# Chunk-selecting attention and a gated FFN on one core: first blocks as 128-token half units, v of the first blocks cast by POOL's DMA queue in one chain with the weights

## The chip, the cores and the metric

The kernel runs on one core of a Trainium2 chip. The metric is the device time of one execution in microseconds; three executions of the kernel before took 316.68, 316.73 and 319.05, median 316.73. A profiled execution gives the trace. Five engines work side by side, each through its own instructions in order: TensorE (PE, matmuls), VectorE (DVE), ScalarE (ACT), GpSimd (POOL) and SyncE (SP, which here only issues DMAs). ACT and POOL issue DMAs too.

## The reference

Inputs are q, k, v of shape (4, 8, 768, 64) in float32 and the weights of a gated FFN (512 to 1536 to 512). Cut to what matters:

```python
k_min, k_max = min and max of k over each chunk of 32 tokens
ub = sum_d max(q * k_min, q * k_max)            # an upper bound per query and chunk
ub = where(chunk of query >= chunk, ub, -1e9)
selected = the 6 chunks of the largest ub
scores = q k^T / 8, masked to selected chunks and to past tokens
attn = softmax(scores) v                        # (4, 8, 768, 64)
x = attn with heads side by side: 3072 tokens x 512
xn = x / sqrt(mean(x^2) + 1e-6) * rms_g
g = xn w_gate;  out = (g * sigmoid(g) * (xn w_val)) w_out
```

A query among the first 128 tokens of a sequence sees at most 4 chunks, so all that it sees are selected.

## The kernel before

The work is cut into 12 blocks of 256 tokens: batch b and block m (0, 1, 2) of its sequence, in the order of the list ORDER (L369, the blocks with m = 0 of all batches first). Each block has two jobs, one for each group g of four heads, then a normalization (`norm`) and an FFN (`ffn`). Block 0 alone (SPLIT) runs its FFN as two pieces of 128 tokens, with its scores cut to match.

A job (`job`) does this. DVE transposes k and q in 32 x 32 squares (L512); ACT or POOL makes bf16 copies of them (L519, L520). DVE reduces k to the minimum and maximum of each chunk (L527); POOL or DVE places these in a block-diagonal tile BD (L539). TensorE multiplies q and its positive part with BD, which gives the bound ub (`upper`, L574). DVE transposes it, takes the sixth largest value (L598) and makes a mask, which a matmul with chunkrow adds to the scores (L654). TensorE computes scores (L643) with the keys on the partitions, ACT the exponential (L693), POOL the triangle of the diagonal blocks (L663). The values matmul (L719) takes v from VX, a bf16 tile with a column of ones, which ACT or POOL casts from vraw (L625, L626). DVE divides by the sum (L734, L738).

`norm` squares the rows on ACT (L754), takes the root on POOL (L760, L762), scales on DVE (L769), transposes on TensorE (L779) and copies with rms_g on DVE or ACT (L788, L792). `ffn` runs gate and value matmuls (L817), 256 tokens wide or, for a piece of 128, with 128 columns and the same number of matmuls; tanh on ACT (L824), products on DVE (L828) and POOL (L839) into hh; or, for some, the last product on DVE (L832). The projection (L849) needs all hh of its tokens and all three thirds of wo. Its result is halved and stored.

k and q come by DMAs on the SP queue (for block 0 half of them on ACT's), v on SP's; each of wg, wv and wo comes in thirds, nine transfers on POOL's queue with a cast to bf16. HELD makes the first load of blocks 2 and 3 wait until a weight third has landed. SP works its issues off in order, so a wait holds the issues behind it, stores among them.

The order of all engines is not written out by hand. A planner (class Plan) gets every operation with an engine or a choice of engines (`flex`), a duration, a priority (due time: attention of a block LEAD = 60 us ahead of its FFN, blocks PACE = 23 us apart), what it reads and writes, and the buffers that it takes. It lists the operations in the order in which they would start. Where TensorE would wait in the first 60 us, it puts matmuls of an identity (L903) that keep it busy.

Of the kernel before, what the change touches and what calls it, by code (L numbers as in the profile page):

```python
# [21 lines left out]
class Op:  # L22
    __slots__ = ("eng", "occ", "lat", "fn", "pri", "deps", "waits", "done",
                 "takes", "uses", "dma", "ready", "mode", "start", "name", "seq", "users", "alts", "after", "inst")

    def __init__(self, name, eng, occ, lat, fn, pri):
        self.name, self.eng, self.occ, self.lat, self.fn, self.pri = name, eng, occ, lat, fn, pri
        self.deps, self.takes, self.uses, self.users, self.after = [], [], [], [], []
        self.dma = None
        self.mode = None  # L30
        self.done = None
        self.alts = {eng: (occ, lat, fn)}


class Rings:
# [34 lines left out]
    def add(self, t, ring, packets, cost, op):  # L70
        self._step(min(t, self.wait[0][0]) if self.wait else t)

        def landed(now, op=op):
            op.done = now + (0.9 if op.dma[2] else 1.2)
        op.done = None
        self.wait.append((t, ring, [packets, cost, landed]))
        self.wait.sort(key=lambda w: w[0])
        self.guess()
# [28 lines left out]
class Plan:  # L107
# [3 lines left out]
    SHARES = ("scale", "swap", "relu", "bd0", "bd1", "dk", "mk")  # L111
    HOP = {"PE": 0.055, "ACT": 0.04, "DVE": 0.04, "POOL": 0.075, "SP": 0.06}
# [37 lines left out]
    def run(self, in_order=(), fill=None):  # L150
# [25 lines left out]
        def est(o, e):  # L176
            t = at[e]
# [28 lines left out]
        while todo:  # L206
            best = None
            for e, c in cand.items():
# [4 lines left out]
                if not rows:  # L213
                    continue
                t0 = max(at[e], min(t for t, o in rows))
                t, o = min(((t, o) for t, o in rows if t <= t0 + 1e-9),
                           key=lambda r: (r[1].pri, r[1].seq))
# [7 lines left out]
            if e == "PE" and fill is not None:  # L225
                begin, cold, end, step, pool, fn = fill
                t0 = max(begin, at[e])
                f = [x for x in self.free[pool] if x[0] + 0.055 <= t0]
# [21 lines left out]
            if o.dma is not None:  # L250
                packets, cost, hw = o.dma
                rings.add(t + o.occ + (0.6 if hw else 1.4), e, packets, cost, o)
# [26 lines left out]
def kernel(  # L279
# [41 lines left out]
    def at(key):  # L321
# [4 lines left out]
    buffers("vraw", 2, [P, 2, NG, 4, D], FP32)  # L326
# [3 lines left out]
    buffers("VX", 20, [P, 2, 4, D + 1], BF16)  # L330
    buffers("qb", 5, [P, 2, BLK], BF16)
    buffers("kx", 3, [P, 2, 2, CB], FP32)
# [13 lines left out]
    buffers("hh", 13, [P, 512], BF16)  # L346
# [22 lines left out]
    ORDER = [(0, 0), (1, 0), (2, 0), (3, 0), (0, 1), (1, 1), (0, 2), (2, 1), (1, 2),  # L369
             (3, 1), (2, 2), (3, 2)]  # L370
    assert sorted(ORDER) == [(b, m) for b in range(B) for m in range(NBLK)]
    PACE, LEAD = 23.0, 60.0
    SPLIT = {0}
    PACKED = {0, 1, 2}
    DIRECT = {(i, hp) for i in range(len(ORDER)) for hp in range(KH) if i >= 6 and hp % 2}

    def HALVES(i):
        return ((0,), (1,)) if i in SPLIT else ((0, 1),)

    def due_attn(i):  # L380
        return PACE * i - LEAD

    def due_ffn(i):
        return PACE * i

    def dma(name, eng, src, dst, packets, cost, pri, writes, takes=(), reads=(), behind=()):
# [11 lines left out]
        o.dma = (packets, cost, eng != "POOL")  # L398
        return o
# [8 lines left out]
    def constants():  # L408
# [25 lines left out]
        for i, t in enumerate(store["VX"]):  # L434
            plan.op(f"ones{i}", "POOL", 0.035, 0.14, lambda t=t: GE.memset(t[:, :, :, D:D + 1], 1.0),
# [6 lines left out]
    HELD = {2: (("wv", 2), ("wo", 1)), 3: (("wo", 1), ("wo", 2))}  # L442

    def load_qk(i, nm, src):
        b, m = ORDER[i]
        key = (nm + "raw", b, m)
        first = True
        for n, a in enumerate((0, 2, 1, 3)):
            eng = ("SP", "ACT")[n % 2] if i == 0 else "SP"
            rows = slice(32 * a, 32 * (a + 1))  # L450
            if i in PACKED:
                sv = src[b].rearrange("(g a) (m r j) d -> a m r g (j d)", a=4, m=NBLK, r=32)[a, m]
                todo = [(sv, lambda rows=rows: at(key)[rows].rearrange("r g j h d -> r g (j h d)"),
                         4, 0.098)]
            else:
                todo = []
                for g in range(NG):
                    sv = src[b, 4 * g + a, BLK * m:BLK * (m + 1), :].rearrange(
                        "(j r) d -> r j d", r=32)
                    todo.append((sv, lambda rows=rows, g=g: at(key)[rows, g].rearrange(  # L460
                        "r j h d -> r j (h d)"), 16, 0.019))
            for k_, (sv, dst, packets, cost) in enumerate(todo):
                dma(f"load {nm}{b}{m}{a}{k_}", eng, sv, dst, packets, cost,
                    loads_due(i, nm == "q"), writes=[key],
                    takes=[(key, nm + "raw")] if first else (),
                    behind=[HELD[i][0]] if i in HELD and first else ())
                first = False

    def loads_due(i, n):
        return -500 + 10 * i + n if i < 2 else due_attn(i) - 30 + n  # L470

    def load_v(i):
        b, m = ORDER[i]
        key = ("vraw", b, m)
        for e in range(2):
            t0 = BLK * m + P * e
            dma(f"load v{b}{m}{e}", "SP", v[b, :, t0:t0 + P, :].rearrange("a p d -> p a d"),
                lambda e=e: at(key)[:, e].rearrange("p g a d -> p (g a) d"),
                64, 0.02, loads_due(i, 2 if i != 1 else -1), writes=[key],
                takes=[(key, "vraw")] if e == 0 else (),  # L480
                behind=[HELD[i][1]] if i in HELD and e == 0 else ())

    def load_w(n, pri, **kw):
        for w, src, nm in ((wg, moe_w_gate, "wg"), (wv, moe_w_val, "wv")):
            dma(f"{nm}{n}", "POOL", src[:, n * TH:(n + 1) * TH].rearrange("(kt p) n -> p kt n", p=P),
                lambda w=w: w[:, :, n * TH:(n + 1) * TH], 32, 0.081, pri, writes=[(nm, n)], **kw)

    def load_wo(n, pri):
        r = slice(n * 4, n * 4 + 4)
        dma(f"wo{n}", "POOL", moe_w_out.rearrange("(kt p) n -> p kt n", p=P)[:, r],  # L490
            lambda: wo[:, r], 32, 0.081, pri, writes=[("wo", n)])

    first_dk = []


    def job(i, g):
        b, m = ORDER[i]
        J = (b, m, g)
        w = 64 if m == 0 else BLK
        nj = w // 64  # L500
        base = due_attn(i) + 0.5 * g
        early = i < 2
        kraw, qraw, vraw = ("kraw", b, m), ("qraw", b, m), ("vraw", b, m)
        kT, qT, kb, qb, kx = ("kT", *J), ("qT", *J), ("kb", *J), ("qb", *J), ("kx", *J)
        bd = ("BD", b, g)

        def turn(nm):
            raw, T = (nm + "raw", b, m), (nm + "T", *J)
            fast = i not in PACKED
            tokens = "p h (j r) -> p j h r" if fast else "p h (r j) -> p j h r"  # L510
            plan.op(f"turn {nm}{J}", "DVE", 0.6 if fast else 0.94, 0.7 if fast else 1.10,
                    lambda: VE.transpose(out=at(T).rearrange(tokens, r=32, j=8),  # L512
                                         in_=at(raw)[:, g]),
                    base + (0 if nm == "k" else 1), reads=[raw],
                    writes=[T], takes=[(T, nm + "T")])

        def half(nm):
            T, hb = (nm + "T", *J), (nm + "b", *J)
            act = lambda: SE.activation(out=at(hb), in_=at(T), func=ACT.Copy)  # L519
            pool = lambda: GE.tensor_copy(at(hb), at(T))  # L520
            flex(f"half {nm}{J}", {"ACT": (0.54, 0.63, act), "POOL": (0.57, 0.61, pool)},
                 base + 2, reads=[T], writes=[hb], takes=[(hb, nm + "b")])
# [3 lines left out]
        for n, op in enumerate((ALU.min, ALU.max)):  # L526
            plan.op(f"ext{n}{J}", "DVE", 0.585, 0.67, lambda n=n, op=op: VE.tensor_reduce(  # L527
                out=at(kx)[:, n], in_=at(kT).rearrange("p h (c t) -> p h c t", t=CH),
                axis=AXX, op=op), base + 1, reads=[kT], writes=[kx],
                takes=[(kx, "kx")] if n == 0 else ())  # L530
        def sub(eng):
            return lambda: eng.tensor_tensor(
                out=at(kx)[:, 1], in0=at(kx)[:, 1], in1=at(kx)[:, 0], op=ALU.subtract)

        first_dk.append(flex(f"dk{J}", {"POOL": (0.175, 0.22, sub(GE)), "DVE": (0.1, 0.16, sub(VE))},
                             base + 2, reads=[kx], writes=[kx]))
        for n in range(2):
            def place(eng, n=n):
                return lambda: eng.tensor_tensor(  # L539
                    out=BD[b, g].rearrange("p t (h c) -> p t h c", h=2)[  # L540
                        :, 2 * n:2 * n + 2, :, CB * m:CB * (m + 1)],
                    in0=at(kx)[:, n].unsqueeze(2).to_broadcast([P, 2, 2, CB]),
                    in1=own[:].unsqueeze(1).to_broadcast([P, 2, 2, CB]), op=ALU.mult)

            flex(f"bd{n}{J}", {"POOL": (0.21, 0.255, place(GE)), "DVE": (0.11, 0.17, place(VE))},
                 base + 2, reads=[kx, "own", bd], writes=[bd, bd + (m,)])
        turn("q")
        half("q")
        qR = ("qR", *J)

        def qr():
            return at(qraw)[:, g].rearrange("p j h d -> p (j h d)")[:, 0:2 * w].rearrange(
                "p (h s) -> p h s", h=2)

        def relu(eng):
            return lambda: eng.tensor_scalar(
                out=qr(), in0=at(qT)[:, :, BLK - w:], scalar1=HUGE, scalar2=0.0,
                op0=ALU.min, op1=ALU.max)
# [378 lines left out]
```

## Time and profile before

| what | value |
|---|---|
| median of three executions | 316.73 us |
| profiled execution | 321.97 us |
| its span in the trace | 320.3 us |
| mean granted TensorE clock in it | 0.989 |
| PE, DVE, ACT, POOL busy | 302.4, 220.5, 216.2, 156.4 us |
| DMA packets | 30.66 MB, of them POOL's queue 4.72 MB |

How to read it: a line of a group gives line, engine, operation, output and inputs by the program's names, count, busy time, mean of one, and the idle time of the engine just before with what ended it. A line of the timeline begins with the start and the length in microseconds. PE's busy time counts pipelined matmuls that overlap, and filler. The profiled execution is about 5 us above the median; its clock fell below full in two stretches.

### The profile page before, as it was taken

To read this page: it belongs to the slowest core of one execution; us is meant where nothing else is said; L and a number is where in the kernel's file an instruction comes from. 1 tells how busy PE (TensorE), PEld (TensorE's weight loads), DVE (VectorE), ACT (ScalarE), POOL (GpSimd) and SP (SyncE) were. 2 spreads that over 40 slices of the span, in tenths; PEclk is the share of its full clock that TensorE was granted. 3 is DMA by queue.
4 is the path that set the end of the run, shared out by engine and by line. 5 is a ranking of instruction groups with operands and counts; after the bars stand their busy time and mean duration, and the time that the engine had idled before them with its cause. 6 is when DMAs were issued, how large, how long until landed. Compare 5 with 4: busy or idle time off the path is not lost.

```text
span 320.3 us, 11960 instructions
## 1 busy us (share of the span) xinstructions
PE 302.4 (94%) x4952; PEld 235.4 (73%) x4952; DVE 220.5 (69%) x599; ACT 216.2 (68%) x393; POOL 156.4 (49%) x287
## 2 busy tenths in 40 slices
PE   8788999979998999879999999999999999999994
PEld 8687886865865877656788687788587688678681
DVE  6877499895998998968956836496465366437360
ACT  2566746974768896496797686679579469665240
POOL 4774493876764777488656353155133114213120
PEclk9999999998999999979999999999999999999999
DMA  8999986576564647775310300100010110010101
GB/s 183 220 239 207 251 160 150 112 197 142 149 134 118 141 109 174 163 165 114 99 39 19 115 5 2 68 3 4 33 37 0 36 37 2 36 35 2 65 2 65
DMA packets 74838, 30.66 MB, mean 96 GB/s; under 512 B 65568, under 2 KB 70176, under 8 KB 74784
## 3 DMA queue, kind: packets, MB, share of 16 engines
q1 hardware_dynamic: 69712, 24.66, 31.5%
q0 software_dynamic: 4752, 4.72, 8.9%
q8 instruction: 39, 0.64, 0.8%
q10 hardware_dynamic: 320, 0.52, 0.6%
q14 instruction: 15, 0.12, 0.1%
HBM read 28.31 MB, written 6.29 MB: 108 GB/s over the span
## 4 chain that ended last, share of the span: by engine, by line
PE 69%; DVE 8%; DMA 7%; SPq 7%; ACT 4%; issue 3%; POOL 1%; DVEq 0%; ACTq 0%
PE F L817 30%; PE F L849 17%; SPq L390 6%; PE F L719 6%; PE S L643 6%; PE S L574 4%; DMA kraw<-in_k_dram 3%; DMA qraw<-in_q_dram 3%; PE S L654 2%; PE F L903 2%; DMA vraw<-in_v_dram 2%; DVE kx L527 2%; PE F L779 1%; DVE tg L828 1%; ACT pt L693 1%
## 5 line engine op out<-in xcount | busy, mean ns | idle before, releaser
L693 ACT ACTIVATE pt<-S 128x1024 bf16<-128x1024 f32 (+3 forms) x100 | 86.2, 887 | 25.8 <-PE S L654 24.8
L839 POOL TENSOR_TENSOR hh<-tg,vs 128x512 bf16<-128x512 bf16 x54 | 62.3, 1157 | 64.1 <-ACT vs L836 40.7
L828 DVE SCALAR_TENSOR_TENSOR tg<-th,F 128x512 bf16<-128x512 bf16 x72 | 48.8, 681 | 44.1 <-ACT th L824 37.9
L817 PE MATMUL F<-xsT,wg 128*128 128x256 bf16 (+1 forms) x624 | 76.0, 267 | 1.7 <-DVE xnat L738 1.7
L817 PE MATMUL F<-xsT,wv 128*128 128x256 bf16 (+1 forms) x624 | 75.8, 266 | 0.5 <-DVE tg L828 0.5
L849 PE MATMUL F<-wo,hh 128*128 128x512 bf16 x288 | 68.2, 381 | 0.0
L817 PEld LDWEIGHTS <-wg 128*128 128x128 bf16 x624 | 56.4, 99 | 10.8 <-issue 2.7
L817 PEld LDWEIGHTS <-wv 128*128 128x128 bf16 x624 | 55.8, 98 | 8.1 <-issue 1.0
L824 ACT ACTIVATE th<-F 128x512 bf16<-128x512 f32 x72 | 43.0, 602 | 15.0 <-PE F L817 13.5
L663 POOL TENSOR_SCALAR_AFFINE_SELECT pt<-pt 128x512 bf16<-128x512 bf16 x48 | 31.2, 654 | 42.8 <-ACT pt L693 42.4
L849 PEld LDWEIGHTS <-hh 128*128 128x128 bf16 x288 | 26.5, 98 | 27.9 <-issue 0.8
L643 PE MATMUL S<-qb,kb 32*128 32x256 bf16 (+1 forms) x784 | 33.3, 257 | 3.3 <-ACT pt L693 2.0
L836 ACT ACTIVATE vs<-F 128x512 bf16<-128x512 f32 x54 | 32.4, 600 | 4.4 <-PE F L817 3.3
L527 DVE TENSOR_REDUCE kx<-kT 128x16 f32<-128x512 f32 x48 | 30.8, 663 | 0.0
L719 PE MATMUL F<-VX,pt 128*128 128x65 bf16 x672 | 26.9, 195 | 3.7 <-ACT vs L836 3.0
L719 PEld LDWEIGHTS <-pt 128*128 128x128 bf16 x672 | 24.9, 99 | 6.0 <-ACT pt L693 2.3
L865 DVE TENSOR_SCALAR osb<-F 128x512 f32<-128x512 f32 x17 | 11.6, 687 | 24.7 <-PE F L849 24.6
L643 PEld LDWEIGHTS <-kb 32*128 32x128 bf16 x784 | 14.0, 92 | 15.5 <-issue 13.7
L903 PE MATMUL F<-ident 128*128 128x128 bf16 x328 | 23.1, 232 | 2.1 <-POOL ident masks.py:199 1.4
L903 PEld LDWEIGHTS <-ident 128*128 128x128 bf16 x328 | 20.8, 105 | 2.8 <-POOL ident masks.py:199 1.4
L654 PE MATMUL S<-mtd,chunkrow 32*128 32x128 bf16 (+2 forms) x384 | 20.9, 204 | 0.6 <-issue 0.6
L654 PEld LDWEIGHTS <-chunkrow 32*128 32x128 bf16 x768 | 19.3, 94 | 2.4 <-issue 1.4
(60 smaller groups left out, 374.4 us busy)
## 6 DMA issues: line engine op xcount, KB each, us to landing
vraw<-in_v_dram SPq DMA_DIRECT2D x24, 256.0 KB, 4.2
out_dram<-osb SPq DMA_DIRECT2D x24, 256.0 KB, 2.1
kraw<-in_k_dram SPq DMA_DIRECT2D x72, 64.0 KB, 2.8
qraw<-in_q_dram SPq DMA_DIRECT2D x72, 64.0 KB, 2.3
wg<-in_moe_w_gate_dram POOLq DMA_DIRECT2D x3, 512.0 KB, 11.9
wv<-in_moe_w_val_dram POOLq DMA_DIRECT2D x3, 512.0 KB, 11.6
wo<-in_moe_w_out_dram POOLq DMA_DIRECT2D x3, 512.0 KB, 17.5
kraw<-in_k_dram SPq DMA_DIRECT2D x10, 128.0 KB, 5.4
```

The lines of the kernel that those rows point to most:

```text
L527: plan.op(f"ext{n}{J}", "DVE", 0.585, 0.67, lambda n=n, op=op: VE.tensor_reduce(out=at(kx)[:, n], in_=at(kT).rearrange("p h (c t) -> p h c ...
L643: TE.matmul(s[a // 2][:, a % 2, c0:c0 + q1 - q0], kbt[r, t, ks], qbt[r, t, q0:q1], start=(t == 0), stop=(t == 1 and not mask), skip_group_ ...
L654: TE.matmul(o, chunkrow[r, BLK * kg + P * e:BLK * kg + P * (e + 1)], mv, start=False, stop=(d == 1), skip_group_check=True)
L693: lambda pt=pt, hs=hs, c0=c0, c1=c1, x=sc[hp]: SE.activation(out=at(pt)[:, hs, c0:c1], in_=at(x)[:, :, c0:c1], func=ACT.Exp, scale=SCALE), ...
L719: TE.matmul(o[:, a, :], p_[:, a, off:off + P], vt[:, e, a, :], start=(kb_ == 0 and a == 0), stop=(kb_ == nkb - 1 and a == 3), skip_group_c ...
L817: TE.matmul(at(p_)[:, n * W:(n + 1) * W], w[:, g, ht * P:(ht + 1) * P], at(xT)[:, g, 0:W], start=(g == 0), stop=(g == NP - 1), skip_group_ ...
L824: plan.op(f"tanh{U}.{hp}", "ACT", 0.48, 0.6, lambda th=th, gp=gp: SE.activation(out=at(th), in_=at(gp), func=ACT.Tanh, scale=0.5), pri, re ...
L828: VE.scalar_tensor_tensor(out=at(tg), in0=at(th), scalar=1.0, in1=at(gp), op0=ALU.add, op1=ALU.mult), pri - 30, reads=[th, gp], writes=[tg ...
L836: plan.op(f"vcopy{U}.{hp}", "ACT", 0.48, 0.6, lambda vs=vs, vp=vp: SE.activation(out=at(vs), in_=at(vp), func=ACT.Copy), pri + 0.1, reads= ...
L839: plan.op(f"hh{U}.{hp}", "POOL", 1.11, 1.16, lambda tg=tg, vs=vs, hh=hh: GE.tensor_tensor(out=at(hh), in0=at(tg), in1=at(vs), op=ALU.mult) ...
L849: TE.matmul(at(op)[:], at(("hh", *U, ht // K))[:, o:o + P], wo[:, ht, :], start=(ht == 0), stop=(ht == NHT - 1))
L903: TE.matmul(store["F"][slot][:, 0:P], ident[:], ident[:], start=True, stop=True)
```

## The change

The list of blocks becomes a list of units. The four blocks with m = 0 are cut into halves of 128 tokens: first the first halves of all four batches, then their second halves, then the eight other blocks whole, in the order of before. A first half needs no bound and no mask; its chunk minima and maxima are computed all the same, but with a due time of the second half. Each half runs its own norm and its own FFN piece with 128 columns. SPLIT is gone; instead the last unit's norm and FFN run in two pieces.

Loads of k and q for the first eight units are one DMA for each head group, with 128 partitions and runs of 1 KB, and a job waits only for its own group. They follow each other on SP in one line (FIRST), unit 0's q on ACT's queue. v of the eight half units isn't loaded to vraw any more: POOL's queue copies and casts it straight into VX. These eight casts and the nine weight thirds form one chain on that queue in the order CAST; for the planner each starts no earlier than 3.5 us before the transfer two ahead is done (AHEAD, `follow`). v0 waits for unit 0's k, the first weights for its q. Loads k3, k4, k5, k6 wait for weight thirds (HELD).

Buffers: vraw 2 to 1, VX 20 to 10 of double size, kx 3 to 8, six new ones kh for half k, hh 13 to 12. The planner gets PATIENT, which on DVE lets a more urgent operation that is soon ready go ahead of a long one; it assumes later SP loads to land 1.5 us later; and the buffers xs and hh are no longer handed out in strict order. A gate matmul waits for both wg and wv of its third.

```diff
+    AHEAD = 3.5
+    PATIENT = {"DVE": 0.6}
...
-            t = at[e]
+            t = max(at[e], o.floor)
+            if o.follow is not None:
+                t = max(t, o.follow.done - self.AHEAD)
...
+                if e in self.PATIENT:
+                    soon = [r for r in rows if r[0] <= t0 + self.PATIENT[e]]
+                    for t, o in now + sorted(soon, key=lambda r: (r[1].pri, r[1].seq)):
+                        end = t + o.alts[e][0] - 0.1
+                        if not any(t < r[0] < end and r[1].pri < o.pri - 10 for r in soon):
+                            break
...
-    buffers("vraw", 2, [P, 2, NG, 4, D], FP32)
+    buffers("vraw", 1, [P, 2, NG, 4, D], FP32)
...
-    buffers("VX", 20, [P, 2, 4, D + 1], BF16)
+    buffers("VX", 10, [P, 2, 2 * 4, D + 1], BF16)
...
-    buffers("kx", 3, [P, 2, 2, CB], FP32)
+    buffers("kh", 6, [P, 2, P], FP32)
+    buffers("kx", 8, [P, 2, 2, CB], FP32)
...
-    buffers("hh", 13, [P, 512], BF16)
+    buffers("hh", 12, [P, 512], BF16)
...
-    ORDER = [(0, 0), (1, 0), (2, 0), (3, 0), (0, 1), (1, 1), (0, 2), (2, 1), (1, 2),
-             (3, 1), (2, 2), (3, 2)]
+    LATE = [(0, 1), (1, 1), (0, 2), (2, 1), (1, 2), (3, 1), (2, 2), (3, 2)]
+    UNITS = [(b, 0, (t,)) for t in range(2) for b in range(B)] + [(b, m, (0, 1)) for b, m in LATE]
...
-    SPLIT = {0}
-    PACKED = {0, 1, 2}
-    DIRECT = {(i, hp) for i in range(len(ORDER)) for hp in range(KH) if i >= 6 and hp % 2}
+    PACKED = {i for i, (b, m, toks) in enumerate(UNITS) if m == 0}
+    DIRECT_FROM = 10
...
+    def pieces(i):
+        toks = UNITS[i][2]
+        return tuple((t,) for t in toks) if i == len(UNITS) - 1 else (toks,)
...
+        o.slack = 1.5 if pri > -30 and eng == "SP" else 0.0
...
-    HELD = {2: (("wv", 2), ("wo", 1)), 3: (("wo", 1), ("wo", 2))}
+    FIRST = "k0 q0 k1 q1 k2 q2 k3 q3 k4 q4 k5 q5 k6 q6 k7 q7".split()
+    CAST = "v0 v1 w0 v2 w1 v3 w2 wo0 v4 wo1 v5 wo2 v6 v7".split()
+    HELD = {"k3": ("wg", 0), "k4": ("wv", 2), "k5": ("wo", 0), "k6": ("wo", 1)}
+    START = {"v0": ("k", 0), "w0": ("q", 0)}
...
+    def cast_v(i, **kw):
+        b, m, toks = UNITS[i]
+        key, e = ("VX", b, m), toks[0]
+        t0 = BLK * m + P * e
+        dma(f"cast v{i}", "POOL", v[b, :, t0:t0 + P, :].rearrange("a p d -> p a d"),
+            lambda: at(key)[:, e, :, 0:D], 64, 0.022, -400, reads=[key] + ones + kw.pop("reads", []),
+            writes=[key + ("h", e)], takes=[(key, "VX")] if not e else (), **kw)
...
+        w = BLK if m else 64 * s0
...
+        later = base if whole or s0 else due_attn(UNIT_OF[b, m, 1]) + 0.5 * g
...
-        base = due_ffn(i) + toks[0]
+        base = due_ffn(i) + (11.5 if toks[0] and m else 0)
...
-                            reads=[xT, (nm, third)], writes=[p_], takes=[(p_, "F")])
+                            reads=[xT, ("wg", third), ("wv", third)], writes=[p_], takes=[(p_, "F")])
...
+    chain = [o for o in plan.ops if o.dma and o.eng == "POOL"]
+    for x, o in zip(chain, chain[1:]):
+        o.after.append(x)
+    for x, o in zip(chain, chain[2:]):
+        o.follow = x
...
-    for o in plan.run(in_order=("kraw", "qraw", "vraw", "kT", "qT", "kb", "qb", "VX", "xsT", "xs", "hh", "xnat"),
+    for o in plan.run(in_order=("kraw", "qraw", "vraw", "kT", "kh", "qT", "kb", "qb", "VX", "xsT", "xnat"),
```

## The prediction

> **What bounds the kernel now.** I read the page's busy line first, then a table of busy time by stretch, then TensorE's timeline where the table shows losses.
>
> ```profile
> PE 302.4 (94%) x4952; PEld 235.4 (73%) x4952; DVE 220.5 (69%) x599; ACT 216.2 (68%) x393; POOL 156.4 (49%) x287
> L817 PE MATMUL F<-xsT,wg 128*128 128x256 bf16 (+1 forms) x624 | 76.0, 267 | 1.7 <-DVE xnat L738 1.7
> L903 PE MATMUL F<-ident 128*128 128x128 bf16 x328 | 23.1, 232 | 2.1 <-POOL ident masks.py:199 1.4
> ```
>
> TensorE is the bound, but "94%" flatters it. The 328 matmuls of L903 are filler, and busy time of pipelined matmuls overlaps. So I priced each form at its step in unbroken runs (the chain lists sixteen 256-column gate matmuls at 1.75 us and 48 of 128 columns at 2.68): 109 ns for 256 columns, 55.8 for 128, 216 for 512, 32.3 for 65; the small score and bound matmuls by their groups. The sum is 263 us in a span of 320.3. About 57 us hold no useful matmul; of these 24 lie in the first 30 us and 5 at 42 to 47. From 150 to 300 us only some 0.5 us in 10 is lost.
>
> ```profile
> 10.00:20.00 10.00, 7.72 (x205) 6.79 (x203) 7.00 (x25) 5.46 (x14) 7.67 (x14) 1.00 1.18 240
> 20.00:30.00 10.00, 8.11 (x226) 7.15 (x226) 8.64 (x29) 6.79 (x17) 6.46 (x16) 1.00 1.24 206
> 30.00:40.00 10.00, 9.40 (x197) 8.95 (x194) 5.00 (x13) 8.31 (x18) 4.82 (x7) 1.00 1.20 243
> 60.00:75.00 15.00, 12.81 (x212) 9.86 (x205) 13.30 (x36) 12.07 (x28) 11.68 (x20) 0.89 0.64 158
> 130.00:150.00 20.00, 16.33 (x241) 12.46 (x239) 15.96 (x41) 14.32 (x27) 14.14 (x23) 0.91 0.74 157
> 150.00:300.00 150.00, 149.84 (x2504) 114.16 (x2503) 88.37 (x262) 106.20 (x180) 55.24 (x82) 1.00 0.10 31
> ```
>
> After the stretch come its length, PE, weight loads, DVE, ACT, POOL, clock, DMA share and GB/s. DMA is saturated to 40 us, while DVE is half idle there; later DMA is nearly idle.
>
> ```profile
> 27.90 1.06 PE L817 MATMUL F<-xsT,wg 128*128 128x128 bf16 x16
> 41.86 4.85 PE L903 MATMUL F<-ident 128*128 128x128 bf16 x84
> 46.55 1.89 PE L849 MATMUL F<-wo,hh 128*128 128x512 bf16 x8
> 48.27 0.61 PE L779 MATMUL F<-ident,xs 128*128 128x128 bf16 x8
> ...
> 128.30 1.05 SPq L390 DMA_DIRECT2D vraw<-in_v_dram  x2
> 134.27 0.63 ACT L626 ACTIVATE VX<-vraw 128x512 bf16<-128x512 f32 x1 [3.31 <-DMA vraw<-in_v_dram]
> 136.35 0.22 PE L719 MATMUL F<-VX,pt 128*128 128x65 bf16 x2 [1.65 <-ACT vs L836]
> 139.70 0.54 PE L719 MATMUL F<-VX,pt 128*128 128x65 bf16 x7 [1.32 <-ACT vs L836]
> ```
>
> The first gate matmul runs at 27.9, and at 41.9 TensorE has gated block 0 and has nothing else: 84 fillers until the first projection (46.55; the last wo third landed at 42.4). Block 1 is turned only at 48.27. At 134 a late v load costs TensorE idle pieces of 1.65, 0.70 and 1.32 us.
>
> [...] the first wv third landed 11.3 us after its issue among q loads, but the next four weight thirds, alone, 2.5 us apart (23.95, 26.46, 29.00, 31.54). [...] packets of 256 bytes took 25 ns each at the start, of 2048 bytes 107 to 120, so half the rate for v. [...] Weight issues took 0.75 to 0.98 us here beside a busy DVE[...]; none of v is in this trace.
>
> **The change part by part.**
> - *Half units first.* The first four units need 128 tokens each, and no selection (their early chunks are all selected): no upper-bound matmul, no top-k. The DVE chain ahead of the first scores shrinks, and 512 KB rather than 1 MB must land. Landings: eight 128 KB transfers of k and q came between 3.63 and 7.39, 0.54 us each; four of v (256 KB) between 7.39 and 13.27, about 1.3. In the changed order, ahead of the first wv third: twelve k/q transfers (6.5 us), two v casts (2.6), two weight thirds (5.0), after 3.1 us of start: 17.2. The chain for unit 0 ends about there too: DVE transposes of three units come before its normalization (about 13), then square 0.82, the two small POOL operations 0.78, scale 0.35, turn 0.40, copy 1.14: some 17. First gates near **18** instead of 27.9.
> - *What TensorE has before wo.* In the changed instruction order 384 gate matmuls of 128 columns (four half units, 21.4 us) precede the first projection, before 192 (10.7); attention ahead of it is 4.3 us, before 4.7. So 25.7 us of useful work instead of 15.4: **-10.3 us**, if wo is there. There are 250 fillers instead of 328, none just ahead of wo. From 18 us, 24 us of work and 2.6 of filler fit.
> - *When the last wo lands.* After 17.2: four more casts (5.2), seven weight thirds (17.5), k and q of units 3 to 6 (8.6; units 3 to 6 are held behind weights, so part may fall later): 48.5, against 46.55 for the first projection now: **+1.95**. Bounds: a cast at half its price gives 44.6 (it writes half the bytes); at twice its price, 56.3.
> - *128-column gates.* 384 pairs of them replace 384 of 256 columns: 384 x (2 x 55.8 - 109.4) ns = 0.84, and 0.09 for more score pieces: **+0.93**.
> - *Switches of TensorE's tiling.* 146 instead of 138 (counted in the order); a pass of scores took 0.1 us more than its columns: **+0.8**. Bounds 0 and 1.6.
> - *The last block in halves.* The end was without gaps and stays so, but the last four projection matmuls now wait for vs 0.60 and POOL's hh 1.16 behind 8 matmuls (1.73): **+0.2**.
> - *v casts leave ACT and POOL*: 8 of 24 are gone, 0.62 us each. At this stage both engines idle a third of the time or more, so I price them at 0; at most 5 us of ACT's time comes free.
> - *DVE*: half transposes (2 x 16 at about 0.58 for 6 at 1.10 and 2 at 0.68) +2.6, extremes in halves +0.6, more xsT copies +6.6, relu +2.7, output copies -3.4, the rest about -0.7: +8.4 us, hidden in the 12.3 us that DVE idles in the first 40. Without that cover up to +8.
> - *The queues moved past.* wg, wv, wo and the casts now sit in POOL's order between triangles, rms and hh; the third wg waits behind unit 0's first hh. SP's first loads go in one line, each held load stopping those behind it. Priced at 0 for the forecast, since two transfers are still in flight; up to 4 us of gaps in the bound.
> - *One vraw buffer, and loads planned 1.5 us later*: SP's order changes around the stall at 134 (3.7 us idle). It may vanish or recur behind the single buffer: I take half, **-1.8**; ends 0 and -3.7.
>
> Sum: -10.3 + 1.95 + 0.93 + 0.8 + 0.2 - 1.8 = -8.2. The profiled execution took 321.97 (span 320.3, 1.7 around it); its clock fell to 0.89 and 0.91 in two stretches, some 3 us, and it is 5.2 above the median. Against its own time: 313.8; against the median 316.73: **308.5**.
>
> **Rivals.**
> *B, better:* wo lands by 46 and the v stall is gone: a further 2.5 + 1.9, **304**. For: the weights alone ran at 2.5 us. Against: 256-byte packets.
> *C, DVE becomes the bound.* From 46.5 to 130 DVE is busy 90% (12.6 of 13.5, 13.3 of 15, 21.6 of 25, 27.4 of 30), and in the first 75 us TensorE already waits for it. If its 8.4 us do not fit early, the gain is handed back at 60 to 130: about **316**. Against: 12.3 us idle before 40.
> *D, slower:* the weight chain. v casts in front of wo cost twice the price (7.8 us), and POOL's in-order queue leaves gaps (4), so wo2 lands at 60 and TensorE, out of hh buffers (12, three for a half unit), stands. It decides from 56.7 for the tie; at 60 it costs 11.8 more than the forecast: **320.3**, slower by 1.1%. For: no v cast is in the trace, and the chain is now paced by compute. Against: thirds alone at 2.5 us show slack.
> That half units bring no earlier start can't be excluded, but then C's figure holds.
>
> **Chances.** Forecast 0.50 (own range 304.5 to 312.5), B 0.20, C 0.14, D 0.16. Range 303 to 319.5, which leaves out most of D and the lower part of B. One per cent is 3.2 us, about what a measurement of this kernel tells from no change: faster than 313.6: 0.72; within: 0.12; slower than 319.9: 0.16.
>
> **What would show it.** First gate matmul at 16 to 20; no filler just ahead of the first wo matmul, which starts at 46 to 51 with 384 gate matmuls behind it; casts landing 1 to 2 us apart between weights; DVE over 80% before 40; 130 to 150 without waits for vraw. Wrong if: the wo thirds land after 56; TensorE waits for DVE at 50 to 130 more than now; POOL's DMA issues grow beyond 1.5 us each; SP's held loads come late.

## The result, and the profile after

The changed kernel takes **338.76 us** (median; 338.08 to 340.28), the kernel before beside it 317.5 (316.68 to 319.05): a ratio of **1.067**, 95% interval 1.061 to 1.073. I had forecast 308.5, with a range of 303 to 319.5. It is slower, and far beyond my rival on the slower side, who said 320.3.

The profiled execution took 338.08 us, its span is 336.3. From its page: the busy line, the granted clock in 40 slices, ACT's DMA queue (packets, MB, share of 16 engines), and the shares of the chain that ended last; below it ACT's queue in the kernel before.

```profile
PE 307.1 (91%) x5281; PEld 246.2 (73%) x5306; DVE 230.8 (69%) x639; ACT 210.6 (63%) x397; POOL 166.8 (50%) x294
PEclk9575999769989999999999999999999999999999
q10 hardware_dynamic: 792, 0.26, 0.3%
PE 66%; DMA 16%; DVE 8%; ACT 3%; issue 2%; SPq 2%; POOL 1%; POOLq 0%; ACTq 0%; DVEq 0%
```

```profile
q10 hardware_dynamic: 320, 0.52, 0.6%
```

TensorE's busy time has not grown much. Its granted clock is 0.949 over the whole span: the trace has it at half for four stretches, 34 us in all (8.9 to 19.2, 22.6 to 32.8, 63.5 to 73.8 and 97.7 to 101.1), against 6.8 us in the kernel before. The table of busy time by stretch (length, PE, weight loads, DVE, ACT, POOL, clock, DMA share, GB/s) shows where TensorE does less; first one line of the kernel before, then the changed kernel:

```profile
0.00:10.00 10.00, 8.56 (x112) 8.56 (x113) 7.09 (x9) 2.85 (x5) 4.21 (x38) 1.00 0.94 191
```

```profile
0.00:10.00 10.00, 6.30 (x70) 6.05 (x70) 5.19 (x8) 3.01 (x6) 4.38 (x27) 0.95 0.22 64
10.00:20.00 10.00, 6.69 (x64) 5.37 (x63) 3.47 (x6) 3.17 (x9) 4.25 (x7) 0.54 1.07 156
20.00:30.00 10.00, 6.52 (x84) 5.55 (x84) 5.70 (x18) 4.19 (x13) 4.11 (x8) 0.63 0.56 90
60.00:75.00 15.00, 10.18 (x185) 9.38 (x181) 11.54 (x36) 6.28 (x14) 8.10 (x19) 0.66 0.72 113
130.00:150.00 20.00, 19.71 (x417) 15.41 (x418) 18.31 (x62) 15.97 (x31) 12.32 (x21) 1.00 0.72 159
150.00:300.00 150.00, 148.09 (x2508) 114.38 (x2517) 109.32 (x297) 107.45 (x179) 67.90 (x109) 1.00 0.19 53
```

In the first 10 us, where only loads are to be done, the DMA engines are a fifth busy and move 64 GB/s (before: 0.94 and 191); from 10 to 30 the clock is near half. From 150 to 300 TensorE is nearly as busy as before (148.09 of 150, against 149.84). With matmuls priced as in the prediction, the time without useful matmul comes to 38.2 us by 50 us (before: 29.9) and 55.3 by 100 (37.3); after 110 the two lose alike. So the loss is in the first 100 us. TensorE's timeline there, and VectorE's waits in the first 70 us (total, times, longest):

```profile
34.68 1.06 PE L883 MATMUL F<-xsT,wg 128*128 128x128 bf16 x16
40.88 2.80 PE L975 MATMUL F<-ident 128*128 128x128 bf16 x47
60.06 1.06 PE L883 MATMUL F<-xsT,wv 128*128 128x128 bf16 x16
68.16 1.89 PE L883 MATMUL F<-xsT,wg 128*128 128x128 bf16 x16
76.02 1.90 PE L915 MATMUL F<-wo,hh 128*128 128x512 bf16 x7
```

```profile
DVE qT L561 <- DMA qraw<-in_q_dram: 10.3, 8, 2.6
DVE kh L561 <- DMA kraw<-in_k_dram: 10.2, 9, 1.9
```

First gates at 34.7 (forecast 18, before 27.9), first projection at 76.0 (forecast 48.5, before 46.55). VectorE stood 20.5 us for k and q, the loads that the half units were to bring sooner; in the kernel before such waits came to 3.1 us in the same time. The weight thirds were late too: the third wg was issued at 38.45 (before at 15.67), and the last wo landed at 69.0.

The first sign of a cause is in ACT's queue. Before, it had 320 packets for four transfers: 64 of data and 16 of completion (4 bytes each) for each. Now it has 792: 528 are rmsg's (512 single elements and 16 completions), which leaves 264 for two q transfers, 128 of data and **4** of completion each. What differs is the form. The kernel before loads one head at a time, and the outermost index counts 32 rows. The changed kernel loads a group of heads with `"a (r j) d -> a r (j d)"`, and the outermost index is `a`, which counts 4. The transfers beside these complete in two parts: of the 16 completions of the first wg third, 12 come from 17.47 to 19.87 and 4 from 26.27 to 26.59, where in the kernel before all 16 come from 14.84 to 17.22. My reading is that 4 of the core's 16 DMA engines carry a transfer by group; the trace does not name the engine of a packet, so this is an estimate from these counts.

### The profile page after: what moved, and what is told of

Read it like the earlier page. It is cut to its first block, busy times and chain, and to the rows that moved or that the text cites. A ratio compares the mean times of both kernels' runs of the same rounds, so it can differ in the third digit from the quotient of the medians.

```text
span 336.3 us, 12641 instructions
## 1 busy us (share of the span) xinstructions
PE 307.1 (91%) x5281; PEld 246.2 (73%) x5306; DVE 230.8 (69%) x639; ACT 210.6 (63%) x397; POOL 166.8 (50%) x294
## 4 chain that ended last, share of the span: by engine, by line
PE 66%; DMA 16%; DVE 8%; ACT 3%; issue 2%; SPq 2%; POOL 1%; POOLq 0%; ACTq 0%; DVEq 0%
PE F L883 27%; PE F L915 17%; DMA qraw<-in_q_dram 10%; PE F L780 6%; PE S L636 6%; PE S L710 6%; DMA kraw<-in_k_dram 3%; PE S L721 2%; DVE xs L835 2%; DVE tg L894 2%; SPq L409 2%; DMA vraw<-in_v_dram 2%; PE F L845 1%; DMA out_dram<-osb 1%; ACT junk L820 1%
## 5 line engine op out<-in xcount | busy, mean ns | idle before, releaser
L883 PE MATMUL F<-xsT,wg 128*128 128x128 bf16 (+1 forms) x816 | 77.5, 246 | 2.9 <-DVE osb L931 2.9
L883 PE MATMUL F<-xsT,wv 128*128 128x128 bf16 (+1 forms) x816 | 76.9, 245 | 0.9 <-DVE tg L894 0.9
L883 PEld LDWEIGHTS <-wg 128*128 128x128 bf16 x816 | 61.7, 100 | 9.6 <-issue 3.7
L915 PE MATMUL F<-wo,hh 128*128 128x512 bf16 x263 | 65.7, 380 | 2.4 <-issue 0.8
L883 PEld LDWEIGHTS <-wv 128*128 128x128 bf16 x816 | 61.5, 100 | 6.6 <-issue 1.7
L890 ACT ACTIVATE th<-F 128x512 bf16<-128x512 f32 x72 | 43.2, 601 | 19.5 <-PE F L883 17.2
L915 PEld LDWEIGHTS <-hh 128*128 128x128 bf16 x288 | 25.7, 98 | 27.9 <-issue 1.0
L710 PE MATMUL S<-qb,kb 32*128 32x256 bf16 (+1 forms) x832 | 35.4, 254 | 9.4 <-ACT pt L750 4.9
L561 DVE STREAM_TRANSPOSE qT<-qraw 128x256 f32<-128x256 f32 (+1 forms) x32 | 21.2, 663 | 11.4 <-DMA qraw<-in_q_dram 11.4
L820 ACT ACTIVATE junk<-xnat 128x512 bf16<-128x512 bf16 x24 | 15.1, 630 | 13.9 <-DVE xnat L800 13.6
L931 DVE TENSOR_SCALAR osb<-F 128x512 f32<-128x512 f32 x12 | 8.2, 687 | 19.8 <-PE F L915 16.2
L800 DVE TENSOR_TENSOR xnat<-F,rden 128x256 bf16<-128x256 f32 x48 | 19.9, 421 | 1.1
```

Source lines behind the costliest of these rows:

```text
L561: lambda: VE.transpose(out=at(T)[:, :, 0:W].rearrange(tokens, r=32, j=J), in_=flat(raw, J)[:, g]),
L710: TE.matmul(s[a // 2][:, a % 2, c0:c0 + q1 - q0], kbt[r, t, ks], qbt[r, t, q0:q1], start=(t == 0), stop=(t == 1 and not mask), skip_group_ ...
L883: TE.matmul(at(p_)[:, n * W:(n + 1) * W], w[:, g, ht * P:(ht + 1) * P], at(xT)[:, g, 0:W], start=(g == 0), stop=(g == NP - 1), skip_group_ ...
L890: plan.op(f"tanh{U}.{hp}", "ACT", 0.48, 0.6, lambda th=th, gp=gp: SE.activation(out=at(th), in_=at(gp), func=ACT.Tanh, scale=0.5), pri, re ...
L915: TE.matmul(at(op)[:], at(("hh", *U, ht // K))[:, o:o + P], wo[:, ht, :], start=(ht == 0), stop=(ht == NHT - 1))
```

## The experiments

**Theory E**: k and q on 4 of 16 DMA engines (the estimate above) are the cause, and what else is queued at those four waits with them (the 4 completions above, 6.4 us behind the other 12). Rivals: **V**, v casts hold the weights up (the mechanism of my rival D); **P**, POOL's pacing and order; **H**, half units in 1 KB runs as such.

*By head again* (here "4, 0.055" is what the planner reckons for the transfer):

```diff
-            for g in range(NG):
-                sv = src[b, 4 * g:4 * g + 4, t0:t0 + 32 * J, :].rearrange(
-                    "a (r j) d -> a r (j d)", r=32)
-                todo.append((g, sv, lambda g=g: flat(key, J)[:, g].rearrange(
-                    "p j h d -> p (j h d)"), 8, 0.075 if i == 0 else 0.055))
+            for a in (0, 2, 1, 3):
+                rows = slice(32 * a, 32 * (a + 1))
+                sv = src[b, :, t0:t0 + 32 * J, :].rearrange(
+                    "(g a) (r j) d -> a r g (j d)", a=4, r=32)[a]
+                todo.append(((0, 1), sv, lambda rows=rows: flat(key, J)[rows].rearrange(
+                    "p g j h d -> p g (j h d)"), 4, 0.055))
```

> The changed kernel with one thing undone: k and q of the half units (and of nothing else) come by head row again, four transfers of 32 partitions for each tensor, instead of two of 128 partitions whose outermost index is the head of the group (4 of them). Half units, their order, the v casts on POOL in the chain with the weights, and the pacing stay. Theory E (four engines): a transfer whose outermost index counts 4 is carried by 4 of the 16 DMA engines, and what POOL queues behind it waits at those four. Then this edit alone restores my forecast: first gate matmul at 18 to 22 us instead of 34.7, last wo third landed at 48 to 54 instead of 69.0, 308 to 315 us. Theory V (v casts): casts ahead of wo hold the weights up, whatever form k and q have: wo at 62 or later, 330 us or more. Theory P (pacing and order on POOL) and theory H (half units in 1 KB runs cost the descriptors): also 330 or more, first gates after 30.

Measured: 319.5 us, 1.005 of before (1.002 to 1.008). ACT's queue now has 848 packets, 528 of them rmsg's: 64 of data and 16 of completion for each of four q transfers, as before.

```profile
q10 hardware_dynamic: 848, 0.26, 0.3%
```

This edit alone takes back 6.2 of the 6.7%; V, P and H, whose parts are all still in it, fall as causes of that. (Each transfer brings rows of both groups, so a job waits for both again: that part of the change is undone with it.) Of E's figures only that of wo2, the last third of wo, was met, 53.0: first gates came at 24.7, not by 22, and 319.5 is above its range and 11 us over my forecast. A second cause is left.

*The kernel before, by group.* In blocks 0 to 2 the loop over heads gives way to:

```diff
+            for g in range(NG):
+                sv = src[b, 4 * g:4 * g + 4, BLK * m:BLK * (m + 1), :].rearrange(
+                    "a (r j) d -> a r (j d)", r=32)
+                dma(f"load {nm}{b}{m}{g}", ("SP", "ACT")[g] if i == 0 else "SP", sv,
+                    lambda g=g: at(key)[:, g].rearrange("p j h d -> p (j h d)"), 8, 0.098,
...
```

> The kernel before with one thing done: k and q of blocks 0 to 2 come in two transfers by head group for each tensor (outermost index 4, runs of 2 KB) instead of four by head (outermost index 32). Nothing else is changed; no v cast on POOL, no half units. Theory E: 12 transfers of 256 KB at 32 packets of 107 ns on each of four engines are 3.4 us each, 13.7 for block 0 alone; first gate matmul at 35 or later instead of 27.9, and the last wo third later by 10 or more, 326 to 336 us. Theories V, P and H: nothing of theirs is in it, 315 to 320.

Measured: 338.4, 1.066 (1.056 to 1.076), first gates at 49.7, last wo at 58.7; the time is 2 us above E's range. The same step done to the kernel before costs as much as the whole change. Its table by stretch, and SP's timeline:

```profile
0.00:10.00 10.00, 8.55 (x112) 8.44 (x112) 3.14 (x4) 1.49 (x2) 3.47 (x36) 1.00 0.31 83
10.00:20.00 10.00, 0.69 (x14) 0.53 (x13) 7.02 (x11) 3.13 (x6) 4.31 (x9) 0.64 0.62 142
```

```profile
2.65 13.76 SPq L390 DMA_DIRECT2D vraw<-in_v_dram  x4
16.46 1.45 SPq L390 DMA_DIRECT2D kraw<-in_k_dram  x2
```

SP needs 13.76 us to issue four v loads that took it 3.56 before, so block 1's k is not even issued until 16.5: here the queue behind the transfers by group stood too.

*Transfers alone.* Phases that each wait for the one before:

```diff
+    phase([by_group(ga8[b], b, g) for b in range(4) for g in range(2)])
+    phase([by_head(ha8[b], b, a) for b in range(4) for a in (0, 2, 1, 3)])
+    phase([by_group(gb4[b], b, g, J=8) for b in range(2) for g in range(2)])
+    phase([(GE, vc[b][:, :, 0:D], v[b, :, 0:P, :].rearrange("a p d -> p a d")) for b in range(4)])
+    phase([third(w1, 0)])
+    phase([third(w2, 1)] + [by_group(gw8[b], b, g) for b in range(4) for g in range(2)])
+    phase([third(w3, 2)] + [by_head(hw8[b], b, a) for b in range(4) for a in (0, 2, 1, 3)])
```

> Transfers alone, nothing computed (zeros are stored): each phase starts when the one before has landed. In order: one 128 KB transfer of q by head group (outermost index 4); the same shape of bytes as two transfers by head (outermost 32); eight by group; sixteen by head (the same bytes); four of 256 KB by group; four v casts on POOL; one weight third; a third with eight by group beside it; a third with sixteen by head beside it. Theory E: eight by group take 14 to 17 us (64 packets of 1 KB on each of 4 engines, some 50 ns each, is 3.2 us for two; eight make 13), sixteen by head 3.5 to 5; 256 KB by group 3.4 each or more; the third beside the groups lands 5 us or more later than alone, beside the heads 2 to 4 later. Theory H (1 KB descriptors as such): both forms take the same within 20%. v casts: 1.3 each by my forecast, 2.1 by the packets' 33 ns.

Its timeline (a phase lasts from its first issue to that of the next) and its table by stretch (length, DVE, POOL, clock, DMA share, GB/s) within the phases by group, by head, and by group with 2 KB runs:

```profile
7.24 7.08 SPq L43 DMA_DIRECT2D ga<-in_q_dram  x8
20.95 7.37 SPq L43 DMA_DIRECT2D ha<-in_q_dram  x16
29.95 2.65 SPq L43 DMA_DIRECT2D gb<-in_q_dram  x4
43.58 3.65 POOL L43 DMA_DIRECT2D vc<-in_v_dram  x4 [43.14 <-DMA gb<-in_q_dram]
51.42 0.76 POOL L43 DMA_DIRECT2D w<-in_moe_w_gate_dram  x1 [4.18 <-DMA vc<-in_v_dram]
56.77 9.66 SPq L43 DMA_DIRECT2D gw<-in_q_dram  x8
73.19 8.99 SPq L43 DMA_DIRECT2D hw<-in_q_dram  x16
83.89 14.10 SPq L91 DMA_DIRECT2D out_dram<-zero  x24
```

```profile
9.00:20.00 11.00, 0.00 (x0) 0.00 (x0) 1.00 0.26 92
22.00:29.00 7.00, 0.00 (x0) 0.00 (x0) 1.00 0.50 139
32.00:43.00 11.00, 0.00 (x0) 0.00 (x0) 1.00 0.24 93
```

1 MB by group takes 13.7 us, that is 1.71 for each 128 KB; by head 9.0, of which 7.4 are SP's issuing, at an engines' share of 0.50, so this form waits for its queue and not for the engines. By group the engines' share is 0.26 with runs of 1 KB and 0.24 with 2 KB, as four busy engines of sixteen would give. From share and GB/s I estimate 46 ns for a 1 KB packet by group and 59 by head. H is out. Two of E's figures were off: by head I had forgotten the issue time, and a third beside the groups landed 7.6 us after its issue, beside the heads 6.5 and alone 5.3, so the thirds suffer less than thought; the groups beside it took 16.4. In the changed kernel the first wg third took 14.3 us from issue to landing (by head 7.8), but the wo thirds 9.5 (by head 7.7, medians): the last wo was late above all because it was issued late, at 59.5 instead of 46.4. The four v casts landed 1.15 us apart (47.41 to 50.86): V has no ground in their price.

*Casts behind wo*, in the changed kernel:

```diff
-    CAST = "v0 v1 w0 v2 w1 v3 w2 wo0 v4 wo1 v5 wo2 v6 v7".split()
+    CAST = "v0 v1 w0 v2 w1 v3 w2 wo0 wo1 wo2 v4 v5 v6 v7".split()
```

> The changed kernel with v4 and v5 cast behind the last wo third instead of ahead of it. Theory V: the two casts are what holds wo up; with their places free, wo2 lands some 17 us earlier (the distance between wo's landings and the casts beside them in the changed kernel), and the time falls by 10 to 17, to 322 to 329. Theory E: a cast of 1024 small packets is 2.1 us over 16 engines, so two make 4 us at the most, and the k and q transfers on four engines go on as before: 334 to 338.

Measured: 340.4, 1.071 (1.065 to 1.077), although wo2 landed at 63.5 instead of 69.0. V falls; E's range (334 to 338) was missed by 2 us, on the slower side.

**The other 11 us.** Three theories: **Q**, weights issued late because of POOL's order; **V** again; **C**, VectorE's bound takes back what the start gains. The trace of the kernel by head shows the third wg issued at 29.42, after POOL had idled 3.98 for the first hh. I took the pacing out:

```diff
-    AHEAD = 3.5
+    AHEAD = 100.0
```

> The kernel with k and q of the half units by head, and with the pacing of POOL's transfers taken out: AHEAD is 100 instead of 3.5, so the 17 transfers on POOL (v casts and weights) stand in one block in its order, ahead of nearly all its other work. Theory Q (POOL's order): what is left between the 319.5 of the kernel by head and my 308.5 is that weights are issued late, the third wg at 29.4 behind the first hh of unit 0, while DMA moves 127 GB/s at 20 to 30 us. Then the last wo third lands at 45 to 49 instead of 53.0, and the time is 309 to 315. Theory C (VectorE and the chain behind it): earlier weights only turn into other waits at 50 to 130 us, 317 to 321. Against both: units 1 and 2 share the DMA engines with the block, and POOL has no time for its triangles until it has issued; should that decide, first gates come at 27 or later and the time is 320 or more.

Measured: 324.5, 1.020 (1.016 to 1.025). wo2 did land at 44.2, even earlier than Q said, and yet it is slower. POOL's timeline:

```profile
15.43 0.74 POOL L409 DMA_DIRECT2D wo<-in_moe_w_out_dram  x1 [1.94 <-DMA wg<-in_moe_w_gate_dram]
30.65 3.56 POOL L809 TENSOR_SCALAR_AFFINE_SELECT pt<-pt 128x512 bf16<-128x512 bf16 x6
```

From the eleventh transfer on, POOL waits at nearly every issue for an earlier transfer to land, and unit 0's causal triangle, queued behind, runs at 30.65 instead of 8.55. These waits are the program's: in the trace the transfers of POOL's queue take eight semaphores in turn, and each issue from the ninth on waits for the semaphore of the one eight ahead (the eleventh, at 15.43, for the third, landed at 15.14). First gates come at 39.8. This was the case written against both theories; Q's remedy is wrong, though not yet its observation.

*By head, casts behind wo*: the CAST line above.

> The kernel with k and q of the half units by head, and v4 and v5 cast behind the last wo third. Theory V (casts in the chain): the last wo third lands 4 us or more earlier than at 53.0, 314 to 317. Theory Q: POOL's order, which still puts wg2 behind the first hh, sets it; wo2 1 to 3 us earlier, 317 to 320. Theory C: the same time within 0.3%.

Measured: 316.9, 0.996 (0.994 to 0.998); wo2 at 48.4. Some 0.9% better than by head alone, as V said; in the last run below the same move brings nothing.

*Without pacing, q of units 1 and 2 by ACT*:

```diff
-            eng = "ACT" if i == 0 and nm == "q" else "SP"
+            eng = "ACT" if i < 3 and nm == "q" else "SP"
```

> As the kernel without pacing, with q of units 1 and 2 issued by ACT instead of SP. Measured alone, sixteen 64 KB transfers by head from one queue took 9.0 us, 7.4 of them for issuing, so SP's queue sets when units 1 and 2 are there: their last q landed at 9.8 and 16.6. Theory I (issue): those land 3 us earlier, first gates 1 to 3 us earlier than without this, time 1 to 3 us less than without pacing alone. Theories Q and C: no change within 0.3%, since POOL's weights, or what VectorE does, set the time from 50 us on.

Measured: 323.5, 1.018 (1.013 to 1.022), and *without pacing, casts behind wo* (both edits as above):

> k and q by head, no pacing, and v4 and v5 behind the last wo third. Theory Q with V: wo2 lands at 42 to 46, 307 to 313. Theory C: 317 to 321, as without pacing.

323.2, 1.016 (1.012 to 1.021). With q on ACT, unit 2's last q landed 4.1 us earlier (12.8 against 16.9), yet first gates came later, at 41.1; with the casts moved they came at 39.6, and neither theory's time was met. Both stand behind the same blocked POOL and tell nothing apart.

*Pacing kept, casts behind wo, q of units 1 and 2 by ACT*:

> k and q by head, v4 and v5 behind the last wo third, pacing kept, and q of units 1 and 2 issued by ACT instead of SP. The written-out order has the first gate matmul planned at 18.9 in the kernel without this edit, and the trace has it at 23.9: VectorE, in its order, turns unit 2's q ahead of the normalization of unit 0, and that q landed at 16 to 17. Theory I (SP's queue issues 24 transfers of 0.47 one after another): unit 2's q lands 2 to 4 us earlier, first gates at 20 to 22, time 313 to 315.5. Theory L (unit 2's loads share the engines with the first weights, whatever queue they are on): first gates at 23 to 25, 316 to 318.

Measured: 316.1, 0.989 (0.982 to 0.996). Unit 2's last q landed at 12.8 instead of 17.2, first gates at 21.9 instead of 23.9: I's mechanism is there, but the interval overlaps that without it, and the times don't tell I from L.

*4 us more reckoned for units 2 to 7* (on top of *By head, casts behind wo*; the planner writes the orders out by its own landing times, and on the chip nothing but these orders changes):

```diff
+            if i in PACKED and i >= 2:
+                o.slack = 4.0
```

> k and q by head, v4 and v5 behind the last wo third, and 4 us more reckoned for the landing of k and q of units 2 to 7, so that in the written-out orders their work stands later and VectorE normalizes unit 0 before it turns unit 2. Theory O (order on VectorE): first gates at 19 to 22 instead of 23.9, the wait for unit 2's q ahead of it gone, the third wg issued earlier behind unit 0's first hh, 312 to 316. Theory C (VectorE bounds 50 to 130 us): first gates earlier, the time within 0.4% of 316.9.

Measured: **310.4**, 0.973 (0.968 to 0.979), first gates at 18.75, wo2 at 43.5: faster than both kernels, and 1.6 us below O's range. Theory O holds in kind; C, which said 316.9 within 0.4%, does not decide. *With q by ACT besides*:

> The two edits before together: q of units 1 and 2 on ACT, and 4 us more reckoned for k and q of units 2 to 7. Theories I and O: first gates at 19 to 21, 310 to 315. Theory C: 315 to 318.

310.4, 0.973 (0.968 to 0.978), first gates 19.7: nothing more. And *the order alone*, casts where the changed kernel has them:

> k and q by head and 4 us more reckoned for k and q of units 2 to 7, with v4 and v5 cast where the changed kernel has them, ahead of the last wo thirds. With those two casts behind wo, this made 310.4 (0.973 of before). Theory O (order alone): the casts cost nothing once the orders fit the landings, 0.972 to 0.976 of before. Theory O with V: each cast ahead of the last wo third delays it, wo2 at 46 to 50 instead of 43.5, 0.980 to 0.990 of before.

Measured: 310.5, **0.975** (0.968 to 0.982); wo2 at 44.8. The casts ahead of wo cost nothing that shows once the order fits; why moving them brought 0.9% before, no run shows. VectorE's timeline and a line of TensorE's, by head first, then with the order mended:

```profile
14.09 1.10 DVE L563 STREAM_TRANSPOSE kh<-kraw 128x256 f32<-128x256 f32 x2 [1.08 <-DMA kraw<-in_k_dram]
16.66 0.63 DVE L563 STREAM_TRANSPOSE qT<-qraw 128x256 f32<-128x256 f32 x1 [1.48 <-DMA qraw<-in_q_dram]
...
18.28 0.33 DVE L837 TENSOR_SCALAR xs<-xnat,ri_all 128x512 bf16<-128x512 bf16 x1
```

```profile
20.39 4.43 PE L977 MATMUL F<-ident 128*128 128x128 bf16 x46
```

```profile
14.73 0.58 DVE L839 TENSOR_SCALAR xs<-xnat,ri_all 128x512 bf16<-128x512 bf16 x1
...
16.99 1.11 DVE L565 STREAM_TRANSPOSE qT<-qraw 128x256 f32<-128x256 f32 x2
```

```profile
15.78 2.73 PE L979 MATMUL F<-ident 128*128 128x128 bf16 x46
```

By head, VectorE waits in its order for unit 2's k and q, and unit 0's normalization, ready since 16.0, stands behind them until 18.28; TensorE then still has 46 fillers in its order, and gates at 24.66. Mended, unit 0 is scaled at 14.73, and the same 46 fillers take 2.73 us instead of 4.43. The clock has a part in this that no run separates: by head it was at half from 17.1 to 24.0 and from 58.1 to 61.5 (0.86 and 0.80 at 10 to 20 and 20 to 30 us, 0.91 and 0.92 at 50 to 60 and 60 to 70), and why it fell no run shows; with the order mended the trace shows no such stretch before 308. POOL's timeline shows the echo, again by head first:

```profile
28.31 1.15 POOL L907 TENSOR_TENSOR hh<-tg,vs 128x512 bf16<-128x512 bf16 x1 [3.98 <-DVE rden L798]
29.42 0.81 POOL L409 DMA_DIRECT2D wg<-in_moe_w_gate_dram  x1
```

```profile
22.00 1.15 POOL L909 TENSOR_TENSOR hh<-tg,vs 128x512 bf16<-128x512 bf16 x1 [0.27 <-ACT vs L906]
23.10 0.82 POOL L409 DMA_DIRECT2D wg<-in_moe_w_gate_dram  x1
```

The third wg is issued behind unit 0's first hh in both. It was 6 us late because the unit was: Q saw a consequence. The edit moves the work of six units on all engines, so no run isolates the swap on VectorE; of the 9 us that it gave, first gates are 5.9 us earlier.

## Why the prediction was wrong

- **Landings: the step that failed.** I took 0.54 us for a 128 KB transfer from eight transfers of the kernel before, by head and from two queues, and gave it to twelve that are laid out otherwise. By group one takes 1.71 alone and 2.05 (16.4 / 8) beside a third. Twelve at 1.71 are 20.5 instead of 6.5 us, which moves my 17.2 for the first wv third to 31.2; it landed at 29.2, and the first gates came at 34.7. The whole diff showed the changed outermost index; what it costs, no trace that I had then shows. With the loads by head the changed kernel takes 319.5 instead of 338.8.
- **The chain of unit 0: failed too, behind the first.** "DVE transposes of three units come before its normalization (about 13)" counted on unit 2 being there; even by head its q lands at 16.6, and the order makes unit 0 wait for it. With the order mended the first gates come at 18.8, near my 18, but by another path: two units are turned ahead of the normalization (at 14.73) and not three. The mended orders as a whole, 1.005 to 0.975, are worth 3.0%, some 9 us.
- **Queues moved past, priced at 0 with up to 4 in the bound.** I named the third wg behind the first hh. By head it was issued 6 us later than with the order mended, but as a follower of the late unit.
- **What TensorE has before wo: right in kind, its size open.** As forecast, 384 gate matmuls of 128 columns precede the first projection. With loads and order mended, the time without useful matmul is 23.6 us by 60 us, before 30.3: 6.7 gained there, where -10.3 and +1.95 make 8.35, and 34.4 against 45.0 by 150 (the 45.0 holds some 3 us lost to half clock, an estimate from 6.8 us at half; 11 projection matmuls without a record make the 34.4 some 2 us too high). 0.975 of 316.73 is 308.8 us (306.6 to 311.0), beside my 308.5. So the sum of the terms came out near, once the two steps above were mended; no run separates them, and errors among them may have cancelled.
- **Last wo: wrong in the changed kernel** (69.0, outside 44.6 to 56.3; I had named a landing after 56 as a sign of being wrong), and at the early end of my bounds with the rest mended (44.8). v casts at 1.3 were near the 1.15 measured, with some luck: the four v transfers that the 1.3 was read from took 5.88 us, which is 1.47 each.
- **DVE +8.4, hidden:** it is +10.3 (230.8 against 220.5). "DVE is half idle" to 40 us read the table too kindly: only from 30 to 40 was it, and from 20 to 30 it was busy 8.64 of 10; nor was DMA nearly idle before 150 (shares of 0.64 and 0.74 in the lines shown). In the mended kernel, from 60 to 150 us, VectorE is busy 83.5 of 90 and TensorE 87.1:

```profile
60.00:150.00 90.00, 87.14 (x1784) 69.12 (x1791) 83.52 (x256) 73.12 (x139) 56.01 (x99) 1.00 0.64 153
```

  Rival C is closer than I had it, but does not decide.
- **The v stall:** gone at 130 to 150 in the changed kernel (19.71 of 20 busy), back ahead of 96 as one wait of POOL for vraw of 5.5 us. Neither end of my price is settled.
- **Rival D** came nearest in the number, 320.3, by a mechanism that two runs (*By head again* and *Casts behind wo*) refute. My range had no case in which k and q themselves are slow: I bounded the v casts, which the trace did not show, but not the new form of the k and q loads, which it did not show either.

Not tried: the mended order with the loads still by group, which would tell how much of 338.8 a planner that knew the true landing times could have hidden. The loads by head also changed what the planner reckons for them, so the 6.2% holds a part of order; the kernel before by group, and the transfers alone, say that it isn't the main part.

## What to carry to other kernels

A duration read from a trace belongs to the layout it was read from: before it is given to another transfer of the same size, compare the outermost index of both sides, and count the completions in the queue's packets. Here 128 KB took 1.71 us by group and 1.13 as two transfers by head, and a share of 0.24 to 0.26 of the DMA engines, where only loads ran, went with four completions for each transfer instead of sixteen. And where orders are written out ahead, an operand that lands late holds up whatever stands behind its user, ready or not (unit 0's normalization, ready at 16.0, stood until 18.28 behind unit 2's k and q); reckoning 4 us more for it gave 3% here.

## What the runs showed of the hardware that I had not expected

- Fewer, larger transfers were slower: 128 KB by group took 1.71 us, two of 64 KB by head 1.13 (9.0 / 8), though the latter waited for a queue that issued one in 0.46 us.
- Issuing itself became slow among transfers by group: four v issues on SP took 13.76 us, 3.56 before; with nothing else on the chip eight issues by group took 7.08 us, 0.89 each; and in the changed kernel two q issues that wait for no semaphore, at 3.78 and 10.93, took 1.46 and 1.25 us, four of k and q from 26.6 on 0.53 each.
- The granted clock of the changed kernel was 0.54 at 10 to 20 us and 0.63 at 20 to 30 (before: 1.00), with fillers in TensorE's order and waits of 0.6 to 2.3 us between them; what sets it, no run shows. And 16 gate matmuls of 128 columns at 68.16, in the third stretch at half clock, took 1.89 us instead of 1.06.
